# Layer 2's DFT over columns folded a second time, and a new order at the layer change

## The chip, the core and the metric

The kernel runs on one core of one Trainium2 chip. The metric is the device time of one execution in microseconds (us), the median of three runs. A core has five engines with queues of their own that work beside each other: TensorE (PE) for matmuls, with weight loads shown apart as PEld, VectorE (DVE), ScalarE (ACT), GpSimd (POOL) and SyncE (SP), which here issues the transfers. Each engine runs its instructions in the order in which the program wrote them; an instruction that needs another engine's result waits for it, and holds up what stands behind it.

## The reference

`x` is 2048 rows by 640 columns. One layer is a Fourier mixing and a gated unit, and the kernel computes two layers:

```
def fourier(x):                   # real part of a DFT over columns, then over rows
    a = x @ dft_hid_re.T          # 640 x 640
    b = x @ dft_hid_im.T
    return dft_seq_re @ a - dft_seq_im @ b    # 2048 x 2048

def gated(x):
    return (sigmoid(x @ w_gate) * (x @ w_up)) @ w_down   # 640 -> 1728 -> 640

for layer in range(2):
    x = x + fourier(layernorm(x))
    x = x + gated(layernorm(x))
```

Inputs and outputs are float32. The kernel gets the accuracy with two float16 parts for each operand (high and low), multiplied in three passes.

## The kernel before

*How the Fourier step is done.* The kernel folds the input over rows and columns, so that it multiplies small matrices: columns d and 640 - d are added or subtracted (`fold_columns`, 321 even and 320 odd columns), and four groups of rows are joined likewise (`fold_rows`, `fold_join`; i = 0 to 3 are four such blocks of rows). `fold_join(i)` has three parts: adds on DVE (L675), a float16 copy on ACT for the high part (L677), and a subtraction on DVE for the low part (L682). One PE step `sequence(i, tp)` then makes the DFT over rows (L796); `tp` is EV or OD, even or odd frequencies. Its sums lie in PSUM, three chunks of 128, 128 and 65 columns, and go through `evict_sums`, an ACT copy (L237) and a DVE subtraction (L239), into the tiles z. `hidden(q, ph)` and `hidden_middle` make the DFT over columns: 18 matmuls each (L922 in `product`), 2 outputs by 3 chunks of z by 3 passes; the moving operand is a 321 column slice of the DFT matrix, "h". Layer 1 has all of this in its opening; in layer 2 it stands at the layer change. `evict_hidden` (L961, L966, L971), `join_hidden` (L996) and `add_hidden` (L1009) bring the result into X; statistics, norm and transposes on PE (L540) follow, and then the products of the gated unit, `gate_up` (L1130).

*The gated unit.* After `gate_up`'s operands come the stretches of `seven(j)`: products of 128 x 512 (L1174), which share a few PSUM banks. The names one, five, two, six, four, three, seven are PE steps; after one, six and seven an ACT copy (L1178, `snap`) takes the sum out of PSUM, and the next product on that bank waits for it. DVE adds (L1224 and L1239), ACT makes the sigmoid (L1181), DVE the product (L1254). The last products go through `down` (layer 1's first half) and `stage` (L1430), evicted by DVE (L1304).

*What sets the order.* All is written by hand. `steps` is a list of PE steps, each with a planned duration; `run(step, jobs)` and `when(t, job)` put the jobs of the other engines between them, at a step or at a planned time. From this one list every engine's queue gets its order. Layer 1's second half computes the folds of i = 0 and 1 in the stretch of `seven` (`f` below, one run of jobs for each block), those of i = 2 and 3 in the last stages. `PLACES` is a table that gives each buffer its place in the one big tile of memory, in the order in which they are taken: an instruction that writes a place waits for the last one that used it.

*Tests.* The kernel checks its DFT matrices for the symmetries that it uses (`load_…`/`test_…`, L1481 to L1511 and others), a small job of two loads, DVE operations and an ACT operation, spread over the run.

Of the kernel before, what the change touches and what calls it, by code (L numbers as in the profile page):

```python
# [17 lines left out]
P = 128  # L18
# [13 lines left out]
EC = EH + 1  # L32
EPS = 1e-5
# [8 lines left out]
XF = 2.0**8  # L42
CS = 2.0**14
ZS = 2.0**-1
# [158 lines left out]
def folded(ctx, tc, pool, dram, big, acc, flag, x, ct, wh, wg, wu, wc, wd, out):  # L203
# [107 lines left out]
    def start_identity():  # L311
        nc.vector.tensor_scalar(ident16, ramp, part[:, 34:35], None, op0=OP.is_equal)

        nc.vector.tensor_tensor(hs, ident16[:, 63:64], ident16[:, 64:65], op=OP.add)
        nc.vector.tensor_scalar(hs, hs, -0.5 * CS, CS, op0=OP.mult, op1=OP.add)
        drop("ramp")
        drop("part")

# [1835 lines left out]
```

## Time and profile before

| | |
|---|---|
| median of three runs | 1105.14 us (1104.71 to 1105.16) |
| the profiled execution's own time | 1106.03 us |
| its span in the profile | 1104.2 us |
| granted TensorE clock | 0.998 |
| PE busy | 1084.0 us, 98% |
| DVE busy | 830.2 us, 75% |
| ACT busy | 572.9 us, 52% |
| POOL busy | 154.6 us, 14% |
| chain that ended last | PE 87%, DVE 8%, issue 2%, DMA 1%, ACT 1% |

The span is one execution from its first to its last instruction; the run's time has some 2 us more around it. "Busy" counts the engine's instructions that calculate. A row of a timeline has a start, a length, the engine, the line in the program, the operation, output and input with partitions x elements, and how many instructions it groups ("x4"); in brackets stands how long the engine was idle before, and what released it. A row of a table by stage has a stretch, its length, and the busy time of each engine with its count of instructions, then the granted clock, the share of the transfers and GB/s. The chain of waits goes back from the last instruction to what released each.

### The profile page before, as it was taken

How to read it: one execution, taken by the hardware profiler on the slowest of the kernel's cores; microseconds unless marked ns; L12 is line 12 of the kernel's file. 1: busy time of each engine (PE TensorE's matmuls, PEld its weight loads, DVE VectorE, ACT ScalarE, POOL GpSimd, SP SyncE). 2: the span in 40 equal slices, each digit the busy share in tenths (PEclk: the TensorE clock that was granted, in tenths of full speed). 3: DMA queues.
4: the chain of work that ended last, by engine and by line, in shares of the span. 5: the costliest groups of instructions: out<-in, count | busy, mean ns of one | idle time of the engine just before them, and what ended most of it. 6: DMA issues, size and time to landing. Idle time of an engine off the chain costs nothing.

```text
span 1104.2 us, 17528 instructions
## 1 busy us (share of the span) xinstructions
PE 1084.0 (98%) x6289; PEld 626.3 (57%) x6289; DVE 830.2 (75%) x1608; ACT 572.9 (52%) x1109; POOL 154.6 (14%) x250
## 2 busy tenths in 40 slices
PE   6999999999999999999999999999999999999997
PEld 3776444457774444457777844444677444444775
DVE  8996789868448999769887569895895356777962
ACT  7776547765315665555225544476761345555520
POOL 3110153312333151000110100012000010000010
PEclk9999999999999999999999999999999999999999
DMA  8414765366996877756742058645569856666521
GB/s 273 155 61 71 199 184 203 115 193 191 251 249 233 251 250 202 235 174 214 229 141 73 1 62 194 200 154 182 185 163 177 265 180 208 202 196 194 190 88 64
DMA packets 183079, 194.70 MB, mean 176 GB/s; under 512 B 76451, under 2 KB 145474, under 8 KB 182982
## 3 DMA queue, kind: packets, MB, share of 16 engines
q1 hardware_dynamic: 182342, 190.87, 58.8%
q0 software_dynamic: 640, 2.62, 0.6%
q8 instruction: 51, 0.84, 0.3%
q14 instruction: 46, 0.38, 0.1%
HBM read 145.29 MB, written 31.91 MB: 160 GB/s over the span
## 4 chain that ended last, share of the span: by engine, by line
PE 87%; DVE 8%; issue 2%; DMA 1%; ACT 1%; POOL 0%; SPq 0%; DVEq 0%; POOLq 0%; ACTq 0%
PE acc L1174 36%; PE acc L1430 17%; PE acc L1130 14%; PE acc L1316 8%; PE acc L922 4%; PE acc L1411 2%; PE acc L1283 2%; PE acc L834 2%; DVE big L642 1%; DMA big<-big 1%; DVE quad L424 1%; DVE big L239 1%; PE acc L796 1%; DVE big L1509 1%; DVE big L594 0%
## 5 line engine op out<-in xcount | busy, mean ns | idle before, releaser
L1174 PE MATMUL acc<-big 128*128 128x512 f16 x2160 | 467.8, 379 | 2.8 <-ACT big L1178 1.9
L1174 PEld LDWEIGHTS <-big 128*128 128x128 f16 x2160 | 211.3, 98 | 257.8 <-issue 3.5
L1430 PE MATMUL acc<-big 128*128 128x320 f16 x1512 | 213.2, 299 | 0.4 <-DVE big L1304 0.4
L1178 ACT ACTIVATE big<-acc 128x512 f32<-128x512 f32 x160 | 94.0, 593 | 191.9 <-PE acc L1174 167.5
L1430 PEld LDWEIGHTS <-big 128*128 128x128 f16 x1512 | 147.9, 98 | 58.5 <-issue 0.6
L1130 PE MATMUL acc<-big 128*128 128x512 f16 (+1 forms) x900 | 156.6, 336 | 0.0
L1130 PEld LDWEIGHTS <-big 128*128 128x128 f16 x900 | 87.9, 98 | 67.7 <-DVE big L239 0.2
L1481 ACT ACTIVATE big<-big 128x768 f32<-128x768 f32 (+6 forms) x106 | 79.0, 745 | 53.2 <-DVE big L1511 17.0
L1304 DVE SCALAR_TENSOR_TENSOR big<-acc,big 128x320 f32<-128x320 f32 x112 | 53.1, 485 | 53.7 <-PE acc L1411 27.2
L239 DVE SCALAR_TENSOR_TENSOR big<-big 128x640 f16<-128x640 f32 (+7 forms) x94 | 75.9, 830 | 22.5 <-ACT big L237 19.4
L1316 PE MATMUL acc<-big 128*128 128x320 f16 x656 | 89.3, 299 | 0.0
L1391 DVE TENSOR_TENSOR big<-big 128x512 f16<-128x512 f32 x126 | 85.3, 688 | 2.3 <-ACT big L1390 2.3
L1390 ACT ACTIVATE big<-big 128x512 f16<-128x512 f32 x126 | 74.0, 618 | 25.0 <-DVE big L1391 11.1
L237 ACT ACTIVATE big<-big 128x640 f16<-128x640 f32 (+9 forms) x94 | 63.8, 707 | 35.7 <-POOL big L1082 15.8
L1316 PEld LDWEIGHTS <-big 128*128 128x128 f16 x656 | 64.2, 98 | 25.1
L1224 DVE TENSOR_TENSOR big<-big,acc 128x512 f32<-128x512 f32 x40 | 27.3, 682 | 44.4 <-PE acc L1174 30.6
L516 ACT ACTIVATE big<-big 128x384 f16<-128x384 f32 (+2 forms) x56 | 36.0, 667 | 36.6 <-DVE big L501 17.2
L1181 ACT ACTIVATE big<-big 128x512 f32<-128x512 f32 x80 | 49.7, 622 | 9.7 <-DVE big L1224 6.6
L386 POOL DMA_INDIRECT out<-big,rows x8 | 8.6, 1070 | 310.9 <-DVE big L1304 173.5
L1509 DVE TENSOR_TENSOR big<-big 128x512 f32<-128x512 f32 x64 | 46.2, 722 | 5.9 <-DMA big<-in_ct 5.7
L1402 DVE TENSOR_TENSOR big<-big 128x512 f32<-128x512 f32 x72 | 50.1, 697 | 0.1
L439 POOL TENSOR_SCALAR rowt<-rowt 128x1 f32<-128x1 f32 x24 | 13.0, 540 | 242.4 <-ACT big L437 242.4
(199 smaller groups left out, 1230.2 us busy)
## 6 DMA issues: line engine op xcount, KB each, us to landing
big<-in_ct SPq DMA_DIRECT2D x256, 128.0 KB
big<-kept_f SPq DMA_DIRECT2D x63, 320.0 KB
big<-kept_S SPq DMA_DIRECT2D x33, 512.0 KB
big<-kept_w SPq DMA_DIRECT2D x33, 320.0 KB
big<-in_ct SPq DMA_DIRECT2D x32, 256.0 KB
big<-kept_G SPq DMA_DIRECT2D x21, 320.0 KB
kept_S<-big SPq DMA_DIRECT2D x13, 512.0 KB
big<-in_wg SPq DMA_DIRECT2D x19, 320.0 KB
```

The costliest lines, as they stand in the source:

```text
L237: nc.scalar.activation(dh, src, AF.Copy, scale=s)
L239: nc.vector.scalar_tensor_tensor(dl, src, s, dh, op0=OP.mult, op1=OP.subtract)
L1130: nc.tensor.matmul(ps, w[wp][:, d * P : (d + 1) * P], xt[:, xp, :], start=(d == 0 and wp == HI and xp == HI), stop=(d == ND - 1 and wp == LO))
L1174: nc.tensor.matmul(ps, wt, xt, start=start and n == 0, stop=n == len(todo) - 1, skip_group_check=not start)
L1178: nc.scalar.activation(dst, ps, AF.Copy)
L1304: nc.vector.scalar_tensor_tensor(xe, ps[:, :EH], CB, xe, op0=OP.mult, op1=OP.add)
L1316: nc.tensor.matmul(held["pd", i, e][0][:, :EH], held["t", half, j].parts[hp][:, i * P : (i + 1) * P], held["w", 2, j].parts[wp][:, e * EH ...
L1390: nc.scalar.activation(h, v, AF.Copy)
L1391: nc.vector.tensor_tensor(l, v, h, op=OP.subtract)
L1430: nc.tensor.matmul(ps[:, :EH], a[n][hp][:, i * P : (i + 1) * P], w[n][:, wp], start=fresh and m == 0, stop=m == len(todo) - 1, skip_group_ ...
L1481: nc.scalar.activation(v, v, AF.Square, accum_out=new_sum()[:p])
L1509: nc.vector.tensor_tensor(bd[:, :, 1], bd[:, :, 0], bd[:, :, 1], op=same)
```

## The change

The second fold: over the 321 columns k of layer 2's folded input, column k and 320 - k are added or subtracted once more (`fold_again`), 161 even and 160 odd sums. The DFT matrix h then has even outputs from one half and odd outputs from the other: of the three chunks of z, two hold only one kind, and their matmuls write every second column of the PSUM sum, 161 or 160 of 321; the third chunk, 65 rows, holds both kinds and keeps 321. Layer 1's Fourier step stays as it was.

```
     def product(ps, ph, r, at, m):
-        for d, (_, n) in enumerate(KT[r]):
-            w = held["h", r, d].f16[:n]
+        for d, (_, n) in enumerate(KT):
+            o, ws = ps[:m, :EC], [w[:n] for w in held["h", r, d].parts]
+            if steps and d < 2:
+                c = (r + d) % 2
+                o, ws = o[:, c::2], [w[:, : HE + 1 - c] for w in ws]
+            ws = [w[:, : o.shape[1]] for w in ws]
...
-                    nc.tensor.matmul(ps[:m, :EC], z[:, at : at + m], w[:, 384 * wp : 384 * wp + EC],
+                    nc.tensor.matmul(o, z[:, at : at + m], ws[wp],

+    def fold_again(to, f, r):
+        c, every = EH - 2 * r, (slice(None),) * (len(f.shape) - 1)
+        for n, to_c, op in ((HE + 1, 0, OP.add), (HE, HE + 1, OP.subtract)):
+            nc.vector.tensor_tensor(to[(*every, slice(to_c, to_c + n))], f[(*every, slice(0, n))],
+                                    f[(*every, slice(c, c - n, -1))], op=op)
```

`fold_join` has four parts now, with `fold_again` between the adds and the ACT copy; the odd half is 321 wide (it was 320, and a small memset on POOL for the last column goes). For i = 3, at the layer change, it runs by halves (`only`), set between the first evictions. The one row that is folded apart (`fold_row`) gets two more operations and a fifth step.

```
-    def fold_join(i, v=ALL, do=(0, 1, 2)):
+    def fold_join(i, v=ALL, do=(0, 1, 2, 3), only=ALL):
...
             if 1 in do:
-                nc.scalar.activation(take_parts(key, i)[:, :, 0, :w], f[:, GB::2], AF.Copy)
+                fold_again(a, b, n)
             if 2 in do:
+                nc.scalar.activation(p[:, :, 0, :EC], a, AF.Copy)
+            if 3 in do:
+                nc.vector.tensor_tensor(p[:, :, 1, :EC], a, p[:, :, 0, :EC], op=OP.subtract)
...
-                [(fold_rows, 1, ALL, (1,))], [(fold_join, ALL, (0,))], [(fold_join, ALL, (1,))],
-                [(fold_join, ALL, (2,))])):
+                [(fold_rows, 1, ALL, (1,))], [(fold_join, ALL, (0, 1))], [(fold_join, ALL, (2,))],
+                [(fold_join, ALL, (3,))])):
```

Layer 2's matrix was layer 1's, stored to memory and loaded again (six transfers each way); it is now loaded from the input and split into its float16 parts anew (eight loads, eight splits on ACT and on DVE), with factors of a half or one by row (`hs2`, eleven small DVE operations in the opening).

```
-        when(t + 60 + 2 * q, load_wh_again, *divmod(q, 3))
+        when(t + 4 + 2 * q, load_wh2, *divmod(q, 3))
+        when(t + 12 + 2 * q, split_wh2, *divmod(q, 3))
```

The order of PE steps at the layer change, with the jobs of DVE and ACT moved along:

```
             order = [(sequence, 0, EV), (sequence, 1, EV), (sequence, 0, OD), (sequence, 1, OD), (sequence, 2, EV),
-                     (sequence, 2, OD), (hidden, 0, 0), (sequence, 3, EV), (hidden, 1, 0), (sequence, 3, OD),
-                     (hidden, 0, 1), (hidden, 2, 0), (hidden, 3, 0), (hidden, 1, 1), (hidden, 2, 1), (hidden, 3, 1),
-                     (hidden_middle,)]
+                     (sequence, 3, EV), (sequence, 2, OD), (hidden, 0, 0), (hidden, 0, 1), (sequence, 3, OD),
+                     (hidden, 1, 0), (hidden, 1, 1), (hidden, 2, 0), (hidden, 3, 0), (hidden_middle,),
+                     (hidden, 2, 1), (hidden, 3, 1)]
...
-    run(he + 2, evictions(0, (EV,)))
+    join = [[(fold_join, 3, ALL, (n,), (k,)) for n in range(1, 4)] for k in range(2)]
+    run(he + 2, [(evict_sums, 0, EV, 0), (fold_join, 3, ALL, (0,)), *join[0], *evictions(0, (EV,))[1:], *join[1]])
```

Six more tests check the new symmetry; two scales change by a half (`XF`, `ZS`), four planned times of later jobs by 2 to 6 us, and all of `PLACES` is new, so that what each instruction waits for before it may write a place is different throughout:

```
-405 80 404 403 81 86 91 96 400 101 395 106 111 116 121 126 390 131 134 384 387 381 140 143 374 369 364 359 354
+80 81 405 404 82 87 92 97 401 102 107 396 391 112 117 386 122 127 130 383 133 380 377 372 367 136 362 357 352
```

Three places in the order of instructions follow. The new kernel's lines have other numbers: there L684 is `fold_again`, L699 the join's add (L675 before), L706 its copy (L677) and L708 its subtraction (L682), L656 the step of `fold_rows` before it (L642); L241 and L239 are a split on DVE and ACT (L239, L237), L1226 the PSUM copy (L1178), L1229 the sigmoid (L1181), L1287 and L1299 the adds behind three and seven (L1239, L1251), L1450 and L1557 test or weight work (L1402, L1509), L1529 a test's sum (L1481).

DVE in the stretch of seven, where i = 1 is joined (layer 1), before:

```order
L1239 TENSOR_TENSOR big<-big,acc_67 128x512
L1391 TENSOR_TENSOR big<-big 128x512
L1251 TENSOR_TENSOR big<-big 128x512
L675 TENSOR_TENSOR big<-big 128x321 x2
L675 TENSOR_TENSOR big<-big 128x320 x2
L1402 TENSOR_TENSOR big<-big 128x512
```

and after:

```order
L1287 TENSOR_TENSOR big<-big,acc_67 128x512
L1439 TENSOR_TENSOR big<-big 128x512
L1299 TENSOR_TENSOR big<-big 128x512
L699 TENSOR_TENSOR big<-big 128x321 x2
L684 TENSOR_TENSOR big<-big 128x2x161
L684 TENSOR_TENSOR big<-big 128x2x160
L699 TENSOR_TENSOR big<-big 128x320 x2
L684 TENSOR_TENSOR big<-big 128x2x161
L684 TENSOR_TENSOR big<-big 128x2x160
L1450 TENSOR_TENSOR big<-big 128x512
```

Four operations of `fold_again` came in, two behind each pair of adds; all that stands behind them on DVE is later by them.

ACT at the same place, before:

```order
L1481 ACTIVATE big,dsum<-big 128x768
L677 ACTIVATE big<-big 128x2x321
L677 ACTIVATE big<-big 128x2x320
L1178 ACTIVATE big<-acc_314 128x512
L237 ACTIVATE big<-big 128x3x320
L657 ACTIVATE big<-big 1x321 x2
```

and after:

```order
L1229 ACTIVATE big<-big 128x512
L706 ACTIVATE big<-big 128x2x321 x2
L1226 ACTIVATE big<-acc_326 128x512
L239 ACTIVATE big<-big 128x3x320
L1529 ACTIVATE big,dsum<-big 128x768
L1229 ACTIVATE big<-big 128x512
```

The copies of the joined fold still stand right ahead of a copy out of PSUM; each now waits for `fold_again` where it waited for the adds.

DVE at the layer change, where the last fold (i = 3) is joined and the first sums are evicted, before:

```order
L642 SCALAR_TENSOR_TENSOR big<-big,quad_77 128x320
L675 TENSOR_TENSOR big<-big 128x321 x2
L675 TENSOR_TENSOR big<-big 128x320 x2
L682 TENSOR_TENSOR big<-big 128x2x321
L682 TENSOR_TENSOR big<-big 128x2x320
L239 SCALAR_TENSOR_TENSOR big<-acc_314,big 128x512
L239 SCALAR_TENSOR_TENSOR big<-acc_66,big 128x512
```

and after:

```order
L656 SCALAR_TENSOR_TENSOR big<-big,quad_78 128x320
L241 SCALAR_TENSOR_TENSOR big<-acc_326,big 128x512
L699 TENSOR_TENSOR big<-big 128x321 x2
L699 TENSOR_TENSOR big<-big 128x320 x2
L684 TENSOR_TENSOR big<-big 128x161
L684 TENSOR_TENSOR big<-big 128x160
L684 TENSOR_TENSOR big<-big 128x161
L684 TENSOR_TENSOR big<-big 128x160
L708 TENSOR_TENSOR big<-big 128x321 x2
L241 SCALAR_TENSOR_TENSOR big<-acc_66,big 128x512
```

The first eviction moved ahead of the join; the other two wait behind the join's first half, the fourth behind both halves.

More of the change, by code (lines that the diff above doesn't have):

```diff
@@ L575, in folds, with doubled @@
         return e, o[:, :, :EH]
+    def doubled():
+        return 0 if steps else EH
     def fold_stats(i, g):
@@ L903, in load_wh, with load_wh2, split_wh2 @@
             nc.sync.dma_start(s[n : n + 1, :EC], wh[r, 0:1, :EC])
-    def load_wh_again(r, d):
-        v = take(3, "h", r, d).f16.rearrange("p (q c) -> p q c", q=2)
-        nc.sync.dma_start(v[: KT[r][d][1], :, :EC], kept["h", r, d])
+    def load_wh2(r, d):
+        s = take(3, "hr", r, d).f32
+        for p, row, n in (((0, r, P),), ((0, 32 + r, P),), ((0, P + r, 33), (33, r, 32)))[d]:
+            nc.sync.dma_start(s[p : p + n, :EC], wh[r, row : row + n, :EC])
+    def split_wh2(r, d, do=ALL):
+        s = held["hr", r, d].f32
+        if d < 2:
+            c = (r + d) % 2
+            v = held["h", r, d] if ("h", r, d) in held else take(2, "h", r, d)
+            h, l = (w[:, : HE + 1 - c] for w in v.parts)
+            split(h, l, s[:, c:EC:2], hs2[:, 0:1] if (r, d) == (0, 0) else CS, do)
+        else:
+            n = KT[d][1]
+            h, l = (w[:n, :EC] for w in (held["h", r, d] if ("h", r, d) in held else take(3, "h", r, d)).parts)
+            for c in range(2):
+                k = (1, 2, 4, 3)[2 * r + c]
+                split(h[:, c::2], l[:, c::2], s[:n, c:EC:2], hs2[:n, k : k + 1], do)
+        if 1 in do:
+            drop("hr", r, d)
     def split_wh(r, d, do=ALL):
-        n = KT[r][d][1]
+        n = KT[d][1]
         v = (held["h", r, d] if ("h", r, d) in held else take(3, "h", r, d)).f16
@@ L947, in drop_hidden @@
             for d in range(3):
-                if ("h", r, d) not in kept:
-                    keep(held["h", r, d].f16.rearrange("p (q c) -> p q c", q=2)[: KT[r][d][1], :, :EC], "h", r, d)
                 drop("z", r, d)
@@ L1567, in test_hidden_rows, with load_hidden_fold, test_hidden_fold @@
         rest.append(b)
+    def load_hidden_fold(r, k):
+        v = room().rearrange("p (g c) -> p g c", g=2)
+        n = 64 if k < 2 else 33 - r
+        for g, (row, d) in enumerate(((r + 64 * k, 1), (EH - r - 64 * k, -1))):
+            nc.sync.dma_start(v[: 2 * n, g, : HE + 1],
+                              bass.AP(wh.tensor, (r * D + row) * D, [[HE, 2], [d * D, n], [1, HE + 1]]))
+    def test_hidden_fold(r, k):
+        n = 64 if k < 2 else 33 - r
+        a, b = (room()[: 2 * n, 512 * g : 512 * g + HE + 1] for g in range(2))
+        for c in range(2):
+            nc.vector.tensor_tensor(b[:, c::2], a[:, c::2], b[:, c::2], op=OP.subtract if c == r else OP.add)
+        rest.append(b)
     def load_hidden_cols(r, j):
```

104 lines of the change are left out of this document (60 added, 44 removed), and 62 rows, old and new, of the table PLACES.

## The prediction

> **What bounds the kernel now.** I read the page's busy times first, then the waits of TensorE (PE), then a table by stage, then single stretches of VectorE (DVE) and ScalarE (ACT). The page:
>
> ```profile
> span 1104.2 us, 17528 instructions
> ...
> PE 1084.0 (98%) x6289; PEld 626.3 (57%) x6289; DVE 830.2 (75%) x1608; ACT 572.9 (52%) x1109; POOL 154.6 (14%) x250
> ```
>
> PE is the bound: 20 of 1104 us are not matmul. So time comes from matmul work taken off PE, or from waits put on it. The waits of PE that this change can touch (what it waited for, us in total, times, longest):
>
> ```profile
> PE acc L1174 <- ACT big L1178: 1.9, 1, 1.9
> ...
> PE acc L796 <- DVE big L239: 0.6, 1, 0.6
> PE acc L922 <- ACT big L971: 0.5, 1, 0.5
> PE acc L1430 <- DVE big L1304: 0.4, 1, 0.4
> ```
>
> They sit in layer 1's stretch of seven products (L1174), at the layer change (L796, L922) and in layer 1's last stages (L1430). The table by stage (stretch; busy us of PE, PEld, DVE, ACT, POOL):
>
> ```profile
> 360.00:400.00 40.00, 40.00 (x187) 18.18 (x186) 39.62 (x74) 23.17 (x42) 10.95 (x14) 1.00 0.83 257
> ...
> 420.00:430.00 10.00, 8.10 (x38) 3.62 (x37) 9.96 (x16) 5.80 (x12) 0.00 (x0) 1.00 0.60 192
> 430.00:440.00 10.00, 10.00 (x48) 4.53 (x47) 9.87 (x17) 5.59 (x11) 3.40 (x3) 1.00 0.96 206
> ...
> 500.00:520.00 20.00, 20.00 (x149) 14.40 (x148) 19.54 (x39) 12.03 (x25) 0.00 (x0) 1.00 0.61 192
> ...
> 571.70:590.00 18.30, 17.74 (x156) 15.54 (x155) 14.22 (x32) 7.73 (x14) 1.44 (x8) 1.00 0.56 180
> 590.00:612.50 22.50, 21.97 (x177) 16.74 (x176) 14.43 (x29) 12.68 (x27) 3.98 (x11) 1.00 0.00 1
> ```
>
> The reader is to see that DVE has nothing free from 360 to 440 us (39.62 of 40, 9.96 and 9.87 of 10), where layer 1's output is folded for layer 2, and that PE stops there for 1.9 us; in the layer change DVE has a fifth to a third free.
>
> **Part 1: the matmuls of layer 2's hidden DFT.** The chain of waits runs over them:
>
> ```profile
> 587.15 1.97 PE acc L796 x18
> ...
> 593.55 14.81 PE acc L922 x108
> ...
> 619.18 1.12 PE acc L540 x20
> ```
>
> A matmul of 321 columns takes 14.81/108 = 0.137 us, one of 256 columns 1.97/18 = 0.109, one of 128 (a transpose, with a weight load of its own) 1.12/20 = 0.056. That is a straight line, 0.42 ns a column and 2 ns; at 161 or 160 columns it gives 0.0695. Layer 2 has nine steps of 18; 108 matmuls become 161 or 160 wide and 54 stay: 108 x (0.137 - 0.0695) = 7.3 us less PE work. No row has a matmul that writes every second column of PSUM. Bounds: 0.0695 (stride is free; a smaller price has no reason) and 0.137 (each column costs two), so 7.3 or 0. I take 0.0695, since the rows go by columns moved alone.
>
> The rows have short matmuls with a weight load each at 0.056 us. The Trainium skill, "TensorE: Matmul & The Clock Gate", section "Back-to-back issue gap", speaks against it: it states about 81 ns for a sustained stream of weight load and matmul at 128 columns. An estimate from that page, some 85 ns at 161 columns, would make the gain 108 x (0.137 - 0.085) = 5.6 us; the trace's 56 ns at 128 columns disagrees.
>
> **Part 2: what the layer change gives back.** Its first and last PE rows, and the DVE rows that count:
>
> ```profile
> 571.66 2.47 PE L796 MATMUL acc<-big 128*128 128x257 f16 x21
> ...
> 612.46 0.38 PE L1130 MATMUL acc<-big 128*128 128x256 f16 x2
> ```
> ```profile
> 577.84 1.69 DVE L675 TENSOR_TENSOR big<-big 128x321 f32<-128x321 f32 x4
> 579.60 1.65 DVE L682 TENSOR_TENSOR big<-big 128x642 f16<-128x642 f32 x2
> 581.16 3.67 DVE L239 SCALAR_TENSOR_TENSOR big<-acc,big 128x512 f16<-128x512 f32 x6
> ```
>
> It lasted from 571.66 to 612.46 us, 40.8, the two waits of 0.6 and 0.5 included. A join add (L675) is 1.69/4 = 0.42 us, an eviction on DVE (L239) 0.61. The last fold (i=3) gains eight fold_again operations of 161 or 160 columns, half a join add each with its fixed part: about 0.24, together 1.9 us on DVE. The first eviction is moved ahead of the join, which ends the wait at 581.3 (0.6 gained). The fourth eviction then ends at 577.84 + 4 x 0.61 + 1.69 + 1.9 + 1.65 (the two L682, now in four pieces) = 585.5, up to 586.2 with the waits for ACT's copies in between. Its bank is what the last chunk of (sequence, 2, OD) writes into; with (sequence, 3, EV) moved ahead (18 matmuls, 1.97), PE gets there at 585.1: a wait of up to 1.1. The nine hidden steps are then 6 x 0.137 + 12 x 0.0695 = 1.66 us long instead of 2.47, and waits of 0.3 (parts of z for hidden (0,1)), 0.4 (a bank that ACT empties behind a row's statistics, before (2,0)) and 0.5 to 0.9 (transposes and (3,1)) come up, worked out in the same manner. End at 606.2 to 606.55 where 612.46 was: 5.9 to 6.3 us gained; I take 5.9. Ends: 0 to 8.4 (nothing; or all new waits hidden and both old ones gone).
>
> **Part 3: the folds of rows i=0 and i=1 in the saturated stretch.** The rows around PE's stop, on ACT, DVE and PE:
>
> ```profile
> 418.96 1.54 ACT L677 ACTIVATE big<-big 128x642 f16<-128x642 f32 x2 [0.56 <-DVE big L675]
> 420.41 0.58 ACT L1178 ACTIVATE big<-acc 128x512 f32<-128x512 f32 x1
> 420.89 0.99 ACT L237 ACTIVATE big<-big 128x960 f16<-128x960 f32 x1
> 423.81 0.97 ACT L657 ACTIVATE big<-big 1x321 f16<-1x321 f32 x2 [1.93 <-DVE big L651]
> 424.81 0.63 ACT L1181 ACTIVATE big<-big 128x512 f32<-128x512 f32 x1
> ...
> 425.82 0.83 ACT L1481 ACTIVATE big<-big 128x768 f32<-128x768 f32 x1
> 426.55 0.19 ACT L1481 ACTIVATION_READ_ACCUMULATOR big<-big 128x1 f32 x1
> 428.97 1.08 ACT L1178 ACTIVATE big<-acc 128x512 f32<-128x512 f32 x2 [2.22 <-DVE big L682]
> ```
> ```profile
> 418.04 1.69 DVE L675 TENSOR_TENSOR big<-big 128x321 f32<-128x321 f32 x4
> ...
> 427.31 1.54 DVE L682 TENSOR_TENSOR big<-big 128x642 f16<-128x642 f32 x2
> 428.78 0.67 DVE L1239 TENSOR_TENSOR big<-big,acc 128x512 f32<-128x512 f32 x1
> ```
> ```profile
> 429.61 2.75 PE L1174 MATMUL acc<-big 128*128 128x512 f16 x12 [1.90 <-ACT big L1178]
> ```
> ```profile
> 429.61 53.90 PE acc L1174 x249
> ```
>
> Before, an ACT copy out of PSUM (L1178) waited 2.22 us for L682, and PE 1.90 us for the copy. That wait is for a piece of memory that the fold had used; the new table of places puts it elsewhere, so the 1.9 us go. What is late next: DVE gains four fold_again for i=0 and four for i=1, of 2 x 161 or 2 x 160 elements each, as long as a join add (0.42): 3.4 us, and two of one row (about 0.25 each, an estimate from the join add's half width): 3.9 us in all, in a stretch with no gap to take them. On ACT the copies of the joined fold (L677, 0.77 each) stand right ahead of the copy that frees the bank of a "seven" product. That copy ended at 420.41 + 0.58 = 420.99; PE needs it 30 matmuls of 53.90/249 = 0.2165 us before it stopped at 429.61 - 1.90 = 427.71, so at 421.2: 0.2 us to spare. Now the second join copy waits until fold_again of i=1 is done: the join adds ended at about 419.7, plus 3.4 is 423.1; two copies' remainder 0.77 and the PSUM copy 0.58 make 424.4 or a little more. PE waits about 3.1 us at 421.2.
>
> A second wait follows: the sigmoid (L1181) on ACT needs L1239, now at 428.78 + 3.9, ending about 433.3; behind it in ACT's queue stand a split copy of 1280 (1.3), the row's two copies (0.97), a test (1.0) and then the PSUM copy (0.58), 437.7 with the sigmoid's 0.6; PE wants it 24 matmuls (5.2 us) behind 427.71, with the 3.1 us of delay at 436.0. So 1.7 more. Together 4.8 where 1.9 was: 2.9 us lost. Ends: 1.9 gained (DVE catches up elsewhere) and 6.3 lost (below).
>
> **Part 4: the rest.** The new loads and splits of layer 2's DFT matrix stand at 504 to 514 us: eight DVE splits, 2 us, in a stretch with 19.54 of 20 us busy, where their users come 60 us later; I cost them at nothing, and if the cover fails, an L1304 is late, at most by these 2 us. Six loads of the old halves and six stores fall away on SyncE's queue, eight loads come: nothing. The fold of i=2 (four fold_again, 1.7 us) falls near the 0.4 us wait of L1430; I take 0.3 lost (0 to 1). In the opening, 11 operations of one column stand ahead of a gap:
>
> ```profile
> 4.81 0.15 DVE L315 TENSOR_SCALAR hs<-hs 128x1 f32<-128x1 f32 x1
> ...
> 7.48 0.83 DVE L593 TENSOR_TENSOR big<-big 128x640 f32<-128x640 f32 x1 [1.48 <-ACT big L363]
> ```
>
> At 0.15 each, as L315, they take 1.65 us, less where they overlap; the gap of 1.48 hides all but 0.2, which I leave out. Six more tests are spread over the run; they take DVE and ACT time at places with room outside 360 to 440: nothing.
>
> **The sum.** -5.9 + 2.9 + 0.3 = -2.7 us. The profiled execution took 1106.03 us, 0.9 above the median of the three runs (1105.14); 1103.3 by the first, **1102.4** by the median, which I predict. What a measurement can tell from no change is 0.2%, 2.2 us, so "faster" begins at 1102.9.
>
> **The rivals.** *The fold's cost is hidden.* In the saturated stretch some DVE rows take twice their usual time, and GpSimd (POOL) works there:
>
> ```profile
> 361.69 1.03 DVE L642 SCALAR_TENSOR_TENSOR big<-big,quad 128x321 f32<-128x321 f32 x2
> ...
> 371.00 1.35 DVE L1254 SCALAR_TENSOR_TENSOR big<-big 128x512 f32<-128x512 f32 x1
> ...
> 412.30 2.22 DVE L642 SCALAR_TENSOR_TENSOR big<-big,quad 128x321 f32<-128x321 f32 x2
> ```
> ```profile
> 371.76 1.31 POOL L1350 TENSOR_TENSOR big<-big 128x320 f32<-128x320 f32 x1
> ```
>
> The same L642 pair took 1.03 us at 361.69 and L1254 half its 1.35; by such differences the slow rows of this stretch add up to some 4 to 5 us (an estimate). If the shifted order makes POOL and DVE meet less, DVE has most of the 3.9 us back, the waits in Part 3 fall to nought, and the time is 1105.14 - 5.9 - 1.9 + 0.3 = 1097.6, or 1099.5 with the old 1.9 left. Against it: POOL's work stays where it was. The Trainium skill, "SBUF — State Buffer", section "Terms", says that these two engines share a port pair, held for a whole instruction, and the loser blocks; the trace's doubled rows agree.
>
> *The strided write costs as the full width* (the slower side). Each of the 108 then takes up to 0.137 us: Part 1 gives 0, the new waits hide behind the longer steps, 0.6 is kept, and the time is 1105.14 - 0.6 + 2.9 + 0.3 = 1107.7. By the same sum it decides against the change by over 0.2% where a matmul takes over 0.0695 + (2.7 + 2.2)/108 = 0.115 us. For it: no row excludes it; against it: rows go by columns.
>
> *DVE's backlog lasts.* Before, DVE waited again for the first time at 441.5 us:
>
> ```profile
> 441.52 0.69 DVE L1224 TENSOR_TENSOR big<-big,acc 128x512 f32<-128x512 f32 x1 [0.49 <-ACT big L1178]
> ```
>
> If the 3.9 us stay beyond it, two more products wait 1.7 each: 1102.4 + 3.4 = 1105.8, no change. For it: 9.87 of 10 us busy at 430 to 440; against it: this wait shows that there is room from there on.
>
> *Short matmuls at 85 ns*: 1102.4 + 1.7 = 1104.1.
>
> **Chances.** The sum with its small terms (1100.7 to 1104.1) 0.42; cost hidden 0.25; backlog lasts 0.18; strided write 0.10; short matmuls 0.05. Faster: all of the second, two thirds of the first and a little of the others, 0.55; slower: the strided write and part of the backlog, 0.14; the same 0.31. The range 1097.5 to 1106.5 takes in all but the strided write and the outer ends; the likeliest case alone is 1100.7 to 1104.1.
>
> **What would show it.** In the profile after: the short matmuls in the chain at 0.07 us each (wrong if over 0.115); the time between first L796 and first gate product 34.5 to 35 us instead of 40.8; PE waits on the PSUM copy in the seven products of 4 to 5.5 us in two pieces, the first right behind the fold's copies of i=1; PE's old wait for DVE L239 gone. I am wrong if the seven products show no wait or one of 6 us or more, or if PE waits in a stage that I cost at nothing, above all at 500 to 530.

## The result, and the profile after

The changed kernel takes **1117.09 us** (1115.77 to 1117.65, four runs) where the kernel before takes 1105.15 beside it: ratio **1.0107**, 95% interval 1.0089 to 1.0124. It is slower by 12 us; forecast was 2.7 us faster, and the range ended at 1106.5.

The page of the changed kernel, to be set against the one before: the span, the busy times, and the group of the 128 x 512 products (its line is now L1222, it was L1174).

```profile
span 1115.8 us, 17618 instructions
...
PE 1088.6 (98%) x6289; PEld 631.9 (57%) x6289; DVE 843.8 (76%) x1663; ACT 575.7 (52%) x1131; POOL 146.2 (13%) x246
...
L1222 PE MATMUL acc<-big 128*128 128x512 f16 x2160 | 472.2, 381 | 9.1 <-ACT big L1226 9.0
```

and that group before:

```profile
L1174 PE MATMUL acc<-big 128*128 128x512 f16 x2160 | 467.8, 379 | 2.8 <-ACT big L1178 1.9
```

PE is busy for 4.6 us more, although 7.3 were to go, and idle for 7.0 more (27.2 of the span, 20.2 before). The same 2160 products take 4.4 us longer; most of that is two spells at a lower clock, shown below. PE's waits after:

```profile
PE acc L1222 <- ACT big L1226: 9.0, 6, 3.6
...
PE acc L1478 <- DVE big L1352: 0.9, 1, 0.9
PE acc L825 <- DVE big L241: 0.8, 1, 0.8
```

Where the span grew is read off PE's timeline at the four marks: the first row product of layer 2, the first gate product behind it, and the start of the second half's products in layer 2. After:

```profile
577.53 2.47 PE L825 MATMUL acc<-big 128*128 128x257 f16 x21
...
617.77 6.71 PE L1178 MATMUL acc<-big 128*128 128x256 f16 x60
...
870.98 119.30 PE L1222 MATMUL acc<-big 128*128 128x512 f16 x552
```

Before, those marks were at 571.66, 612.46 and here:

```profile
860.07 149.73 PE L1174 MATMUL acc<-big 128*128 128x512 f16 x693 [0.90 <-DMA big<-big]
```

| stretch | before | after | difference |
|---|---|---|---|
| start to the first row product of layer 2 | 571.66 | 577.53 | +5.9 |
| the layer change | 40.80 | 40.24 | -0.6 |
| first gate product to the second half's products | 247.61 | 253.21 | +5.6 |
| from there to the end of the span | 244.1 | 244.8 | +0.7 |
| sum | 1104.2 | 1115.8 | +11.6 |

So three things are to be explained: a layer change that won nothing, a loss in layer 1, and a loss in layer 2's products that the prediction does not have at all.

*The layer change.* In the chain of waits the matmuls that write every second column stand like this (L972; 12 of each 18 are 161 or 160 columns wide):

```profile
597.64 1.97 PE acc L825 x18
599.61 14.75 PE acc L972 x108
...
615.48 2.46 PE acc L972 x18
```

14.75/108 = 0.137 us each, as long as the 321 columns before. Of the two old waits here (0.56 and 0.53 us) the second is gone; in place of the first stands the one of 0.8 (L825) of the list above.

*Layer 1.* PE's timeline in the stretch of seven has four waits, 4.9 us together, where before had one of 1.9:

```profile
393.73 11.81 PE L1222 MATMUL acc<-big 128*128 128x512 f16 x54 [1.06 <-ACT big L1226]
406.27 11.81 PE L1222 MATMUL acc<-big 128*128 128x512 f16 x54 [0.72 <-ACT big L1226]
419.22 5.34 PE L1222 MATMUL acc<-big 128*128 128x512 f16 x24 [1.14 <-ACT big L1226]
426.57 33.60 PE L1222 MATMUL acc<-big 128*128 128x512 f16 x146 [2.01 <-ACT big L1226]
```

ACT's timeline ahead of the last of them shows the mechanism that was forecast: the copy of the joined fold (L706) waits for `fold_again` (L684), and the copy out of PSUM (L1226) stands behind it:

```profile
425.29 0.75 ACT L706 ACTIVATE big<-big 128x642 f16<-128x642 f32 x1 [1.07 <-DVE big L684]
425.94 0.58 ACT L1226 ACTIVATE big<-acc 128x512 f32<-128x512 f32 x1
```

The table by stage adds what was not forecast. After the wait of 2.01 us the granted clock (the column behind POOL) is 0.50 for 3.2 us; behind the wait of 1.90 us in the kernel before it was 1.00. After, then before:

```profile
427.60:430.80 3.20, 3.20 (x9) 1.10 (x8) 3.20 (x5) 1.75 (x4) 0.00 (x0) 0.50 0.49 176
```
```profile
429.60:432.80 3.20, 3.19 (x15) 1.46 (x15) 3.10 (x7) 2.95 (x5) 0.00 (x0) 1.00 0.61 180
```

Half the clock for 3.2 us is 1.6 us lost.

*Layer 2's products.* One wait of 3.58 us; DVE had waited 6.08 us for the load of a test (L1614 is `test_hidden_rows`, an old one), the tests' operations on ACT wait for DVE, and the copy out of PSUM comes late. DVE, ACT and PE:

```profile
755.61 0.49 DVE L1614 TENSOR_TENSOR big<-big 128x320 f32<-128x320 f32 x1 [6.08 <-DMA big<-in_wh]
```
```profile
756.13 0.47 ACT L1529 ACTIVATE big<-big 128x320 f32<-128x320 f32 x1 [4.63 <-DVE big L1614]
...
761.14 0.58 ACT L1226 ACTIVATE big<-acc 128x512 f32<-128x512 f32 x1
```
```profile
761.77 20.62 PE L1222 MATMUL acc<-big 128*128 128x512 f16 x87 [3.58 <-ACT big L1226]
```

The clock falls again behind it: 0.55 from 761.7 to 765.0 us, 1.5 us lost. With the wait that is 5.1 of the 5.6 us of the table.

### The profile page after: what moved, and what is told of

It reads as the page before. It is cut to its first block, busy times and chain, and to the rows that moved or that the text cites. A ratio compares the mean times of both kernels' runs of the same rounds, so it can differ in the third digit from the quotient of the medians.

```text
span 1115.8 us, 17618 instructions
## 1 busy us (share of the span) xinstructions
PE 1088.6 (98%) x6289; PEld 631.9 (57%) x6289; DVE 843.8 (76%) x1663; ACT 575.7 (52%) x1131; POOL 146.2 (13%) x246
## 4 chain that ended last, share of the span: by engine, by line
PE 73%; DMA 11%; DVE 8%; ACT 3%; SPq 2%; issue 1%; POOL 1%; DVEq 0%; ACTq 0%
PE acc L1222 29%; PE acc L1178 14%; PE acc L1478 12%; PE acc L1364 8%; DMA big<-in_ct 6%; PE acc L972 4%; PE acc L1459 2%; PE acc L863 2%; PE acc L1331 2%; DMA big<-kept_f 1%; DMA big<-kept_S 1%; SPq L1550 1%; DMA big<-kept_w 1%; DMA big<-in_x 1%; DVE big L1439 1%
## 5 line engine op out<-in xcount | busy, mean ns | idle before, releaser
L1222 PE MATMUL acc<-big 128*128 128x512 f16 x2160 | 472.2, 381 | 9.1 <-ACT big L1226 9.0
L1222 PEld LDWEIGHTS <-big 128*128 128x128 f16 x2160 | 212.2, 98 | 267.4 <-issue 15.8
L1478 PE MATMUL acc<-big 128*128 128x320 f16 x1512 | 213.5, 299 | 1.5 <-DVE big L1352 0.9
L1478 PEld LDWEIGHTS <-big 128*128 128x128 f16 x1512 | 147.9, 98 | 60.0 <-issue 2.1
L1226 ACT ACTIVATE big<-acc 128x512 f32<-128x512 f32 x160 | 93.0, 591 | 148.8 <-PE acc L1222 147.8
L1178 PE MATMUL acc<-big 128*128 128x512 f16 (+1 forms) x900 | 156.5, 336 | 0.0
L1178 PEld LDWEIGHTS <-big 128*128 128x128 f16 x900 | 88.0, 98 | 67.6
L1529 ACT ACTIVATE big<-big 128x768 f32<-128x768 f32 (+6 forms) x112 | 81.1, 724 | 83.2 <-DVE big L1559 32.1
L241 DVE SCALAR_TENSOR_TENSOR big<-big 128x640 f16<-128x640 f32 (+9 forms) x97 | 78.3, 830 | 14.4 <-ACT big L239 14.4
L239 ACT ACTIVATE big<-big 128x640 f16<-128x640 f32 (+11 forms) x97 | 64.6, 695 | 33.6 <-POOL big L1130 11.9
L1557 DVE TENSOR_TENSOR big<-big 128x512 f32<-128x512 f32 x64 | 45.2, 706 | 17.8 <-DMA big<-in_ct 17.7
L1229 ACT ACTIVATE big<-big 128x512 f32<-128x512 f32 x80 | 49.7, 622 | 12.7 <-DVE big L1272 8.2
L1272 DVE TENSOR_TENSOR big<-big,acc 128x512 f32<-128x512 f32 x40 | 27.2, 680 | 30.7 <-PE acc L1222 21.4
L1450 DVE TENSOR_TENSOR big<-big 128x512 f32<-128x512 f32 x72 | 50.2, 698 | 0.0
L526 DVE TENSOR_TENSOR big<-big 128x384 f16<-128x384 f32 (+2 forms) x56 | 41.4, 750 | 8.0 <-ACT big L525 7.9
```

The costliest lines, as they stand in the source:

```text
L239: nc.scalar.activation(dh, src, AF.Copy, scale=s)
L241: nc.vector.scalar_tensor_tensor(dl, src, s, dh, op0=OP.mult, op1=OP.subtract)
L1178: nc.tensor.matmul(ps, w[wp][:, d * P : (d + 1) * P], xt[:, xp, :], start=(d == 0 and wp == HI and xp == HI), stop=(d == ND - 1 and wp == LO))
L1222: nc.tensor.matmul(ps, wt, xt, start=start and n == 0, stop=n == len(todo) - 1, skip_group_check=not start)
L1226: nc.scalar.activation(dst, ps, AF.Copy)
L1450: nc.vector.tensor_tensor(o, a, b, op=op)
```

## The experiments

The theories: **A**, a matmul that writes every second column costs as much as one of the full width. **B**, the tests stand closer than before (by the program's plan 4.10 us apart in layer 2's first products, 4.45 before: six more tests in less time), so that one is due before its load has landed. **C**, the second fold of blocks 0 and 1 finds no free VectorE time in layer 1's stretch. **D**, a wait of PE of some 2 us or more is followed by a spell at half the clock. The rival to B and C is the new table of places, which makes other instructions wait.

### Columns side by side: theory A

```
-                o, ws = o[:, c::2], [w[:, : HE + 1 - c] for w in ws]
+                o, ws = o[:, HE + 1 :] if c else o[:, : HE + 1], [w[:, : HE + 1 - c] for w in ws]
```

The third chunk's matrix is stored in the same order, and `add_hidden` reads the result with another access pattern (even and odd columns apart), as many operations as before. In this run the new pattern was also used in layer 1, for blocks 2 and 3, where the sums are not reordered; the operations are the same. In all later kernels it is used in layer 2 alone.

> The changed kernel, but the sums lie in PSUM with the 161 even columns first and the 160 odd ones behind, so that each of the 108 short matmuls writes columns that stand side by side; the reordering is done in the last add into X, in as many operations as before. Theory A (a matmul that writes every second column pays for the full width, 0.137 us; written side by side it costs 0.07): the step of 18 falls from 2.46 to about 1.66 us, the time from the first row product of layer 2 to the first gate product from 40.2 to 34.5 to 36, and the run from 1117.1 to about 1111.5. Rival (a short matmul is held at 0.137 by something else, its weight load or the sum it adds to): 18 still take 2.46 us and the run stays at 1117.

Measured: 1110.52 us, ratio to before 1.0055 (1.0037 to 1.0072), 6.6 us under the changed kernel. The layer change lasts 34.72 us, 5.5 less; the other 1.1 us lie outside it, where theory A says nothing. Its chain shows the short matmuls at 3.35/36 = 0.093, which is 1.67 us for each 18 (54 wide ones at 0.137 in 162):

```profile
591.42 3.35 PE acc L973 x36
```

For 18 that is six at 0.137 and twelve at 0.071. Theory A holds, and the estimate by columns (1.66 us) was right for columns that stand side by side.

The same on the kernel before, without anything else of the change:

```
+                    if steps and d < 2:
+                        c = (r + d) % 2
+                        o, wo = o[:, 161 * c : 161 + 160 * c], wo[:, : 161 - c]
```

> The kernel before, with one edit: the matmuls of two chunks of layer 2's DFT over columns move and write only 161 or 160 columns, side by side (the other columns of those chunks are left out of the sum). Theory A: 108 matmuls at 0.07 instead of 0.137 take 7.3 us off PE; the old order of the layer change gives back 1 to 2 of it, so 1098.5 to 1100. Rival (VectorE and ScalarE, which empty the sums, bound the layer change): 2 us or less, above 1103.

Measured: 1104.1 us, ratio 0.9989 (0.9979 to 0.9998), 1 us gained: the rival's number. In the old order the gain goes into waits for VectorE and ScalarE. PE's timeline:

```profile
602.79 0.45 PE L540 MATMUL acc<-ident,big 128*128 128x128 f16 x5 [0.98 <-ACT big L463]
604.79 1.35 PE L540 MATMUL acc<-ident,big 128*128 128x128 f16 x15 [1.55 <-DVE big L465]
607.47 3.39 PE L926 MATMUL acc<-big 128*97 128x161 f16 x18 [1.33 <-ACT big L975]
```

3.9 us of waits for the norm's parts and an eviction, and behind them 18 matmuls in 3.39 us, at a granted clock of 0.50. The layer change is 39.1 us here, 40.8 before, 40.2 with the new order and matmuls at the full price, 34.7 with the new order and short ones: only in the new order (with the join by halves that goes with it) did the short matmuls pay here.

### Layer 1's second fold left out: theory C

```
-            if 1 in do:
+            if 1 in do and i > 1:
                 fold_again(a, b, n)
```

> The changed kernel without the second fold of blocks i = 0 and 1 (eight VectorE operations of 0.51 us in layer 1's stretch of seven; those blocks go on with the unfolded sums). Theory C (these operations, in a stretch where VectorE has no free time, make the copies of the fold late, and with them the copies out of PSUM): PE's four waits of 4.9 us there fall to 1 or less and the half clock behind the last one goes: 5 us less, 1112. Rival (the waits come from the new places or the shifted tests): they stay above 3.5 us and the run above 1115.5.

Measured: 1111.79 us, ratio 1.007 (1.0051 to 1.0089), 5.3 us under the changed kernel. Layer 1 keeps three waits, and the clock stays at 1.00:

```profile
416.54 17.00 PE L1222 MATMUL acc<-big 128*128 128x512 f16 x78 [1.15 <-ACT big L1226]
434.84 6.63 PE L1222 MATMUL acc<-big 128*128 128x512 f16 x30 [1.30 <-ACT big L1226]
442.00 42.25 PE L1222 MATMUL acc<-big 128*128 128x512 f16 x195 [0.53 <-ACT big L1226]
```

3.0 us of waits instead of 4.9: that lies between theory C and its rival. With the second fold 2 us of the waits go, and the lost clock; what makes the other 3.0 is something else. That the time meets the forecast of 1112 is in part luck: in the profiles the stretch from the first product of layer 1's second half to the first row product of layer 2 lasts 245.9 us in the changed kernel, 242.0 here, 239.9 before. So 3.9 us are won where the theory says, and the rest elsewhere.

### The tests as before the change: theory B

The six new tests are left out, and the second span of the tests ends where it did:

```
-    more += [(load_hidden_fold, test_hidden_fold, (r, k)) for r in range(2) for k in range(3)]
...
-(start_of(0, "d", 0) + 76, start_of(0, "e") - 20, 0.55)
+(start_of(0, "d", 0) + 76, start_of(0, "e"), 0.55)
```

> The changed kernel without the six added tests, and with the old end of the tests' second span, so that the tests stand as far apart as before the change; two buffers have another place. Theory B (closer tests use their loads before these have landed; VectorE waits, and behind it ScalarE's copies out of PSUM): PE's wait of 3.6 us at 761.8 us and the half clock behind it go, 5.6 us less, and of layer 1's four waits (4.9 us) perhaps 1: 1110 to 1111.5. Rival (the new table of places makes the loads late): the wait at 761.8 stays and the run at 1116 to 1117.

Without these tests the table of places as it was leaves no room for every buffer, and for that version there is no time; hence the two other places.

Measured: 1108.21 us, ratio 1.0028 (1.0017 to 1.004): 8.9 us under the changed kernel, more than forecast. PE's waits on the copies out of PSUM are two, both in layer 1:

```profile
PE acc L1190 <- ACT big L1194: 3.2, 2, 2.9
```

The wait of 3.58 us in layer 2 is gone, with the places almost untouched (of the table's 919 entries two have another value and three another position), and so is a third of layer 1's. So the six tests, or the closer distance that comes with them, make these waits; the run takes both away at once and can't tell them apart. What is left in layer 1 is 3.2 us and the half clock behind the longest. That this is the second fold's alone is not shown: no run leaves out both the fold and the tests.

One step of theory B has to be put more narrowly. A load that is late by 5 to 6 us is not new: the kernel before has one in the same stretch of layer 2, and so have this one and `spread_tests_2`, which comes further down. DVE's rows, in this order:

```profile
770.78 0.49 DVE L1566 TENSOR_TENSOR big<-big 128x320 f32<-128x320 f32 x1 [5.08 <-DMA big<-in_wh]
```
```profile
774.46 0.49 DVE L1582 TENSOR_TENSOR big<-big 128x320 f32<-128x320 f32 x1 [5.58 <-DMA big<-in_wh]
```
```profile
761.10 0.49 DVE L1599 TENSOR_TENSOR big<-big 128x320 f32<-128x320 f32 x1 [6.00 <-DMA big<-in_wh]
```

In the first two, PE waits for nothing: the load is late at the very end of these products. In the third it is late in their midst, as in the changed kernel, and PE waits 0.27 us. What differs there is what stands behind the test on ACT. In `spread_tests_2` the copies out of PSUM come right behind the test's operation (761.62):

```profile
762.09 1.55 ACT L1211 ACTIVATE big<-acc 128x512 f32<-128x512 f32 x3
```

In the changed kernel two splits, the sums of a norm, a sigmoid, another copy and another test's sum stood between them, and the copy that PE waited for came only at 761.14, 5 us behind the test's operation at 756.13. That this order is what decides is read off these rows; no run changes it alone. There are also more late loads in the changed kernel: DVE's waits of over 1.5 us for loads of tests between 700 and 785 us add up to 19.8 us, against 7.8 before and 9.0 here. Distance by itself does not decide either: in layer 2's second half the plan of the changed kernel puts the tests 3.73 us apart (4.05 before), and PE waits there for one copy only, 0.48 us.

### How long a wait costs the clock: theory D

In the kernel before, small copies on ACT are put ahead of eight copies out of PSUM, so that PE waits:

```
         def six_post():
+            for n in range({1: 20, 3: 24, 5: 28, 28: 22, 30: 26, 32: 30, 34: 32, 36: 34}.get(sixes[0], 0)):
+                nc.scalar.activation(dsum, dsum, AF.Copy)
+            sixes[0] += 1
```

> The kernel before, with 20 to 34 small copies (about 0.2 us each) put ahead of eight of ScalarE's copies out of PSUM, far apart, so that PE waits there for about 0.8, 1.2, 1.6, 2.0, 2.4, 2.8, 3.2 and 3.6 us. Theory D (a wait of about 2 us or more halves the granted clock for some 3 us behind it, which costs 1.5 us more): the longer waits are followed by matmuls at half the clock, those under about 1.9 us are not. Rival (the half clock in the changed kernel came from several waits in a row, or from something else): single waits of 2 to 3.6 us are followed by a full clock.

The waits came out longer than meant; 1151.29 us for the run, which has no meaning by itself. PE's timeline gives for six of the eight waits the time of the 108 matmuls behind them (behind the other two, of 6.50 and 6.04 us, fewer follow):

```profile
175.15 23.47 PE L1175 MATMUL acc<-big 128*128 128x512 f16 x108 [1.25 <-ACT big L1179]
203.29 25.16 PE L1175 MATMUL acc<-big 128*128 128x512 f16 x108 [4.66 <-ACT big L1179]
...
896.54 23.47 PE L1175 MATMUL acc<-big 128*128 128x512 f16 x108 [1.93 <-ACT big L1179]
923.31 25.16 PE L1175 MATMUL acc<-big 128*128 128x512 f16 x108 [3.30 <-ACT big L1179]
954.09 25.42 PE L1175 MATMUL acc<-big 128*128 128x512 f16 x108 [5.62 <-ACT big L1179]
985.82 24.92 PE L1175 MATMUL acc<-big 128*128 128x512 f16 x108 [6.31 <-ACT big L1179]
```

After 1.25 and 1.93 us: 23.47, the full clock. After 3.30 us and more: 1.5 to 2.0 us longer, and no longer for a wait of 6.3 than for one of 3.3. Theory D holds for waits of 3.3 us. Below that, the other runs show that length alone does not decide. The changed kernel's 2.01 us cost the clock, but a wait of 1.14 us stood 5.3 us before it; three waits of 3.9 us together within 6 us cost it in the short matmuls on the kernel before. Single waits are in `spread_tests`, `short_old_tests` and `spread_tests_2`, all three described below:

```profile
425.12 60.38 PE L1207 MATMUL acc<-big 128*128 128x512 f16 x279 [2.64 <-ACT big L1211]
```
```profile
423.88 62.06 PE L1207 MATMUL acc<-big 128*128 128x512 f16 x279 [2.79 <-ACT big L1211]
```
```profile
334.03 91.67 PE L1207 MATMUL acc<-big 128*128 128x512 f16 x414 [2.24 <-DMA big<-kept_w]
```

After 2.64 us the same 279 matmuls take 1.7 us less than after 2.79: the clock stayed at 1.00 (427.0 to 430.4 us). After 2.24 us it was 0.60 for 3.4 us (335.0 to 338.4), and the 414 matmuls take 2.0 us more than at 0.2165 each. In the opening a wait of 1.64 us of the changed kernel is followed by 0.51 (28.1 to 31.5 us), one of 2.00 us in the run without layer 1's second fold by 1.00. So no bound on the length of a wait fits all runs; when it falls, or what came before it, must count too. What exactly does, stays open. The price can also be higher: behind a wait of 3.45 us in the run with the columns side by side the clock was 0.59 for 6.8 us (754.6 to 761.4), 2.8 us lost.

### Together

The two edits that won most, columns side by side and the tests as before the change:

> The changed kernel with the sums side by side in PSUM (reordered in the last add of layer 2), without the six added tests and with the tests as far apart as before the change; two buffers have another place. If the causes add up: 1117.1 - 6.6 (contiguous) - 8.9 (old_tests) = 1101.6, range 1100 to 1103, under the kernel before by some 3.5 us; in the profile the change between layers lasts 34.7 us, one wait of about 3 us is left in layer 1's products. Rival (with shorter matmuls the two edits meet the same wait, so that their gains overlap): 1104 or more.

Measured: 1102.74 us, ratio 0.9982 (0.9973 to 0.9991). The gains add up, within 1.1 us; the layer change takes 35.8 us and not 34.7, since PE waits 1.0 us there for an eviction. PE's waits on the copies are layer 1's alone:

```profile
PE acc L1207 <- ACT big L1211: 3.2, 2, 2.8
```

The same with the remaining tests moved out of layer 1's stretch (a quarter of the pace there, 1.0 behind it):

> short_old_tests (sums side by side, without the six added tests) with the remaining tests moved: a quarter instead of 0.55 of the pace in layer 1's saturated stretch, 1.0 right behind it, the rest as before the change. If layer 1's last waits (3.2 us and the half clock behind, 1.6 us) come from VectorE having no free time there, they go and the run is at 1102.7 - 4.5 = 1098, 1097 to 1099.5. Rival (the tests are not what fills it, or wait where they go): 1101.5 or more.

Measured: 1103.08 us, ratio 0.9981 (0.9968 to 0.9993), nothing won. Layer 1's waits fell to 2.1 us and the clock stayed full there, but new waits came behind it: 1.05 us for a load at 503 and 1.4 us for L1337 (the eviction in the down products) at 568 to 572. The rival was right.

Four kernels keep all six new tests and all of the work, and have the columns side by side and the tests spread by other weights; a kernel differs from the next in these weights alone, and in a place or two. The spans of the one that did best:

```
+    fs, e1 = start_of(0, "j", 1, 0) + 22, start_of(0, "d", 1)
+    spans = [(start_of(0, "d", 0) + 6, start_of(0, "d", 0) + 38, 0.4), (start_of(0, "d", 0) + 38, start_of(0, "d", 0) + 76, 0.3),
+             (start_of(0, "d", 0) + 76, fs, 0.55), (fs, fs + 88, 0.25), (fs + 88, e1, 1.0), (e1, e1 + 30, 0.45),
+             (e1 + 30, start_of(0, "e") - 20, 0.6),
+             (start_of(1, "c", 1, 0) + 5, start_of(1, "j", 0, JC), 0.9), (start_of(1, "j", 0, JC), start_of(1, "d", 0) - 7, 0.93),
+             (start_of(1, "d", 0) + 6, start_of(1, "d", 0) + 58, 0.45),
+             (start_of(1, "j", 1, 0), start_of(1, "j", 1, 0) + 50, 0.7),
+             (start_of(1, "j", 1, 0) + 50, start_of(1, "d", 1), 1.05), (start_of(1, "d", 1), start_of(1, "d", 1) + 30, 0.7)]
```

> The changed kernel with all of its work and all its tests, and two edits: the sums side by side in PSUM (even columns, then odd ones; reordered in the last add of layer 2), and the tests spread in another way: a quarter instead of 0.55 of the pace in layer 1's saturated stretch, more of them right behind it and in layer 2's second half, 0.95 instead of 1.0 in layer 2's first products; two buffers have another place. If the three causes hold (theory A: 5.5 us of short matmuls; theory C: no free time on VectorE in layer 1's stretch, 5 us; theory B: tests too close, 5.6 us): 1117.1 - 16 = 1101, with a range of 1099 to 1103, under the kernel before (1105). Rival: tests that are moved make new waits where they go, or the waits come from the places: 1105 or more.

Measured: 1112.51 us, ratio 1.007 (1.0056 to 1.0085). Layer 1's wait is 0.16 us and the layer change 34.74 us, as forecast; the tests that were moved to layer 2's second half wait there:

```profile
PE acc L1207 <- ACT big L1211: 7.3, 9, 1.8
...
PE acc L1463 <- DVE big L1337: 3.8, 4, 2.1
```

> The changed kernel with all of its work and tests, the sums side by side in PSUM as in short_old_tests, and the tests spread anew: a third instead of 0.55 of the pace in layer 1's saturated stretch, more just behind it and in stretches of layer 2 with free VectorE time, and in layer 2's two runs of products no closer than before the change (4.4 and 4.0 us apart where before had 4.45 and 4.05). Theory (waits come where tests stand closer than before, and in layer 1's stretch where VectorE is full): layer 1's waits fall under 1 us, layer 2's products have none over 0.5 us, 1099 to 1101. Rival (a stretch that has more tests than before waits in its turn, as in combined): waits of 2 us or more in layer 2, 1102.5 to 1106.

Measured: 1105.87 us, ratio 1.0009 (0.9998 to 1.0019). One wait of 2.64 us in layer 1, and 1.29, 1.21 and 1.37 us in layer 2 at 771, 788 and 841 us.

> spread_tests (all tests, sums side by side) with the weights moved once more: a quarter of the pace in layer 1's saturated stretch, 0.45 instead of 0.6 in layer 2's first down products, where spread_tests had waited. Theory (each stretch holds so many tests and no more): layer 1's wait of 2.6 us and layer 2's waits for VectorE (1.3 and 1.4 us) go: 1099 to 1102. Rival (106 tests are too many, wherever they stand): other waits come, 1104 or more.

Measured: **1102.08 us, ratio 0.9966 (0.9955 to 0.9977)**: faster than the kernel before by 0.34% and than the changed one by 15 us. It is the best of four placements of the same work, which took from 1102.08 to 1112.51 us. The waits in layer 1 and 2 are 0.45, 1.25 and 0.27 us; a new one of 2.24 us at 334 us is for a weight (`kept_w`), behind tests that were put between layer 1's halves.

> spread_tests_2 (all work and all tests, sums side by side, tests spread anew) without the tests between layer 1's two halves, where spread_tests_2 waited 2.2 us for a weight's load and had half the clock behind it; they stand in layer 2 now. Theory (the tests' loads there made the weight late): the wait and the slow clock go, 2 to 4 us: 1098 to 1100.5. Rival (the tests wait where they go in layer 2): 1101.5 or more.

Measured: 1110.45 us, ratio 1.0052 (1.0038 to 1.0066). The wait for the weight is gone, but the whole row of tests shifts when some of them move, and two others came late: 4.09 us for `kept_f` at 505 us, and 4.18 us at 704 us, where DVE waited for a test's load:

```profile
701.75 0.49 DVE L1599 TENSOR_TENSOR big<-big 128x320 f32<-128x320 f32 x1 [5.79 <-DMA big<-in_ct]
```
```profile
703.95 73.72 PE L1207 MATMUL acc<-big 128*128 128x512 f16 x333 [4.18 <-ACT big L1211]
```

So the theory that each stretch holds so many tests and no more is not enough: by these rows it depends on where a load is late, and on what stands behind the test in the queues.

## Why the prediction was wrong

In the span the forecast was 2.7 us less, measured were 11.6 more: 14.3 apart. Of these, 5.3 are the layer change (5.9 expected, 0.6 won), 5.6 the wait and the clock in layer 2's products (expected: nothing), 2.7 layer 1 (2.9 and 0.3 expected, 5.9 lost) and 0.7 the end of the run.

**The strided write (Part 1).** The step that failed is "I take 0.0695, since the rows go by columns moved alone". The upper bound, 0.137, was the price, measured at 0.137. The prediction had this as a rival with a chance of 0.10, worked out at -0.6 us for the layer change; measured -0.6. That the figures meet so closely is in part luck: the rival lets the wait for the eviction go and hides all new ones, and a wait of 0.77 us was there. No row showed a strided write, and rows of another kind were given too much weight. The Trainium skill, "PSUM — Partial Sum Buffer", section "Specifications (TRN2)", says that PSUM has lines of 8 bytes and that a pattern which is not contiguous slows matmuls significantly; the runs agree (0.137 us against 0.071). The prediction did not weigh it.

**Short matmuls at 85 ns.** The rival worked out from the Trainium skill, "TensorE: Matmul & The Clock Gate", section "Back-to-back issue gap", is not borne out: side by side they took 0.071 us.

**The layer change (Part 2).** Right once the columns stand side by side: 34.72 us where the prediction looked for 34.5 to 35. Waits of 0.77, 0.80 and 0.50 us came up, 2.1 in all, where the prediction's own list adds up to 2.3 to 2.7. In the changed kernel itself the last two hid behind the longer steps, as the rival had it; the first did not, so the sign that PE's wait for an eviction on DVE would be gone did not come.

**The stretch of seven (Part 3).** The mechanism was right, and the sum of the waits by chance almost exact (4.9 against 4.8), but they were four and not two. Only the one of 2.01 us stands where the prediction put its first (3.1 us); its second, 1.7 us behind the sigmoid at 436 us, did not come; and a part of the waits was the tests' (3.2 us were left with the old tests, 3.0 without the second fold). An operation of `fold_again` took 0.51 us, not 0.42. The term was mis-sized at 2.9 us where the stretch up to the layer change lost 5.9: 3.0 in these waits, 1.6 in the clock, 0.5 more in the wait of L1478 (0.9 after, 0.4 before), which Part 4 had at 0.3; the other 0.8 is not assigned. The lost clock was in no term.

**The rest (Part 4).** "they take DVE and ACT time at places with room outside 360 to 440: nothing" is the step that cost most. With the six tests left out, 8.9 us came back. What made PE wait was not the time of the tests' operations but a load that landed late: the test waits on DVE, and behind it stand copies out of PSUM on ACT. Of the 11.6 us of the span, 5.6 are the stretch of layer 2 with one such wait (3.58) and the half clock behind it. A row of the page before had the hint: DVE's L1509, a test, had 5.9 us of idle time, 5.7 of it for loads; the same group has 17.8 after. And L1566, the kind of test whose load is late by 6.08 us after the change, had waited 5.08 us once before it. The sign that PE waits in a stage costed at nothing came, at 758 us and not at 500 to 530.

**The hidden cost.** The rival by which POOL would give DVE time back did not come: the waits stayed, and DVE's busy time from 300 to 440 us rose from 117.5 to 124.5.

Whether the new table of places has a share in layer 1's waits is not shown: it can't be exchanged for the old one, since the buffers differ.

## What to carry to other kernels

A matmul's price went by the columns that it moves only where its output columns stood side by side (0.071 us against 0.137); put the halves into two blocks and reorder where the result is read anyway. That the operations of background work (here the tests) fit does not make it free when it has loads of its own: what counted here is when its load lands, which queues it blocks when the load is late, and how soon a copy that PE needs stands behind it there. A wait of PE should be priced with the half clock that can follow it: here mostly 1.5 to 2 us more. It followed each wait of 3.3 us and over in the products, and shorter ones only at times: 1.64 and 2.24 us cost it, 1.93 and 2.64 did not.

## What the hardware showed that was not expected

- A matmul of 161 columns that writes every second column of PSUM took 0.137 us, as long as 321 columns side by side; 161 side by side took 0.071.
- Behind a wait of 2.24 us the granted clock was 0.60 for 3.4 us, behind one of 2.64 us in another run it was 1.00; behind one of 1.64 us it was 0.51, behind one of 1.93 us 1.00. Waits of 3.3 to 6.3 us in one run all cost 1.5 to 2.0 us. The Trainium skill, "TensorE: Matmul & The Clock Gate", section "What's actually happening", has the clock fall after an idle window of about 3.4 us; here shorter waits were enough at times, and once 3.9 us in three pieces.
- Moving a few of 106 tests moved the run between 1102 and 1112.5 us, with the same work in it. A load late by 6.08 us cost PE a wait of 3.58 us in one order, one late by 6.00 us a wait of 0.27 in another.
